# An S4D convolution beside a gated GLU: another way to the modes' exponential and angle, and skip weights first in their PSUM bank

## The chip, the cores and the metric

The kernel runs on one core of a Trainium2 chip. A core has five engines that run their own instruction queues side by side: TensorE (PE, with its weight loads PEld), VectorE (DVE), ScalarE (ACT), GpSimd (POOL) and SyncE (SP, which here only issues DMAs). Each queue is worked through in the order in which it was written. The metric is the device time of one execution in microseconds (us).

## The reference

The input x (2048 tokens, 448 channels) is normalised over its channels, and three terms are added: x itself, a state space convolution (branch A) and a gated linear unit (branch B).

```python
dt = jnp.exp(log_dt)
A = -jnp.exp(log_A_real) + 1j * A_imag
C = (C_real + 1j * C_imag) * dt[:, None]
P = jnp.exp((A * dt[:, None])[:, :, None] * pos[None, None, :])
K = 2.0 * jnp.einsum("dn,dnl->dl", C, P).real        # 448 x 2048, from 256 modes each
y = irfft(rfft(u_t, 2 * L) * rfft(K, 2 * L))[..., :L]
...
A_out = y + u * D_skip
h = sigmoid(xn @ w_gate) * (xn @ w_up)               # 1792 wide
return x + A_out + h @ w_down
```

For branch A each channel has 256 modes. Every mode has a magnitude that falls with the position, by exp(log_A_real) and dt, and a phase that grows with it. The complex weight C gives each mode a starting magnitude and a starting angle.

## The kernel before

Two streams of work are written as Python generators, `conv()` for branch A and `glu()` for branch B, and the main loop takes from whichever is further behind its share. A planner then fixes one order of instructions for every engine before the run, with a model of the times of its own. What is marked `hp` goes before other work as soon as the planner takes it for ready; `tc.issue_after` puts an instruction behind another one on its engine. On the chip each engine follows that order and waits where an input is late.

Branch B takes 14 columns of 128 of the hidden layer, in groups, and two halves of the tokens. `gate` does 22 matmuls for one column and 512 tokens into two PSUM tiles `gu` (L705). ACT makes `th` by Tanh from the first (L713), DVE makes `hf` from `th` and the second (L716), ACT rounds it to `hh` (L721), DVE takes the rest `hl` (L723). At the end of a group the matmuls `po` (L818) multiply with the down weights, and DVE adds the result to `acc` (L823). `po` and `gu` share four PSUM buffers (`tag="gu", bufs=4`). New weights come into `wraw` by DMA, ACT rounds them to `wh` (L755), DVE takes the rest `wl` (L759).

Branch A has three stages. `prep` works on the modes, in two halves of 224 channels (112 partitions, 512 modes on each), step by step in turn with the other half. In `exp` it computes the exponential of log_A_real and log_dt: the argument is clamped (L305), split into a whole power of two `ki` (L307) and a rest `fr` (L311 and L312), the rest goes through a Taylor polynomial of degree seven (L314 and six times L316), and the power is put into the exponent bits (L317, L318). ACT then makes Tanh and Exp of the results. For the angle of C, with a3 and b3 the absolute values of its parts, it divides the smaller by the larger (reciprocal on DVE in pieces of 128 columns, L322), takes Arctan on ACT after a table load (L375), and mends the octant and the signs (L385 to L391). Sine and cosine come from ACT (L386, L387). The phases go out to `ph_d`, in parts that matmuls can take without loss.

`kgen` then makes the kernel K in 56 chunks of 8 channels. For each chunk PE spreads the phases (`tr`, L538), ACT takes sines (`S`, L544 to L547), POOL makes powers of the magnitudes (`me`, `mf`, L516), DVE multiplies to `Et` and `Ft` (L598 to L600), and 64 small matmuls add up the modes into the PSUM bank `ko` (L612), four chunks to a bank. At the end of the fourth chunk one more matmul adds the skip weights `dm` to column 0 of each block (L622, in two passes), and ACT copies the bank to `ks` (L625). There is one `ko` bank, so the next group's first matmul into it waits for that copy. `spectra` multiplies the spectra and turns them back into the output.

Matmuls into PSUM add to what is there unless `start` is set, in which case they begin anew.

Of the kernel before, what the change touches and what calls it, by code (L numbers as in the profile page):

```python
# [21 lines left out]
N = 256  # L22
# [2 lines left out]
NB = 64  # L25
NK1 = 33
TWO_PI = 2.0 * math.pi
MAGIC = 1.5 * 2.0**23
NFT = F // 128
WK = 5.5  # L30
# [8 lines left out]
CP = D // 4  # L39
# [91 lines left out]
def s4d_glu_kernel(ctx, tc, io):  # L131
    nc = tc.nc
    hp = tc.high_priority
    v = nc.vector
# [16 lines left out]
    const = ctx.enter_context(tc.tile_pool(name="const", bufs=1, side="left"))  # L151
    ident = const.tile([128, 128], F32, name="ident")
    wx = const.tile([128, 64], F32, name="wx")
    wk = const.tile([128, 2, 128], F32, name="wk")[:, :, :64]
    hpi = const.tile([128, 1], F32, name="hpi")
    nc.gpsimd.memset(hpi, math.pi / 2)
    one = const.tile([128, 1], F32, name="one")
# [5 lines left out]
    dm = const.tile([128, D // 32, 8], F32, name="dm")  # L163
# [3 lines left out]
    junk = const.tile([128, 1], F32, name="junk")  # L167


    lim = const.tile([128, 2, 3], F32, name="lim")  # L170
    nc.gpsimd.memset(lim, -1.0)

# [127 lines left out]
                nc.scalar.dma_start(x1_d[:, r : r + 9 : 8], x1s_[p][64 * i : 64 * i + 64])  # L300
        yield 2 * WX

    def exp(ex, ki, fr, pl):

        v.tensor_scalar(ex, ex, lim[:CP, 0, 1:2], lim[:CP, 0, 2:3], ALU.min, ALU.max)  # L305
        yield
        nc.scalar.activation(ki, ex, AF.Identity, scale=1.0 / math.log(2.0))  # L307
        yield
        ln2h = 0.693359375
        ln2l = math.log(2.0) - ln2h  # L310
        v.scalar_tensor_tensor(fr, ki, -ln2h, ex, ALU.mult, ALU.add)  # L311
        v.scalar_tensor_tensor(fr, ki, -ln2l, fr, ALU.mult, ALU.add)  # L312
        cs = [1.0 / math.factorial(i) for i in range(8)]
        nc.scalar.activation(pl, fr, AF.Identity, scale=cs[7])  # L314
        for i in range(6, 0, -1):
            v.scalar_tensor_tensor(pl, pl, cs[i], fr, ALU.add, ALU.mult)  # L316
        v.tensor_scalar(ki, ki, 127.0, 8388608.0, ALU.add, ALU.mult)  # L317
        v.scalar_tensor_tensor(ex, pl, 1.0, ki.bitcast(F32), ALU.add, ALU.mult)  # L318

    def pieces(t):  # L320
        for i in range(0, 2 * N, 128):
            v.reciprocal(t[:, i : i + 128], t[:, i : i + 128])  # L322


    SF = [CP, 2 * N]
    three = lambda t: t[:, : 2 * N].rearrange("p (t n) -> p t n", t=2)
# [14 lines left out]
    def prep(pool, h, srcs):  # L341

        cr, ci, aim, ex = srcs
        new = lambda n, sh=SF, dt=F32: pool.tile(sh, dt, name=n, bufs=2)
        a3, b3, m3, w3, s3 = (new(n) for n in ("a3", "b3", "m3", "w3", "s3"))
# [6 lines left out]
        yield from exp(ex, ki, fr, pl)  # L352
        for i, c in enumerate((0.5, -1.0, 1.0 / TWO_PI, 2.0)):
            nc.scalar.activation(hdt[:, i], ex[:, 2 * N :], AF.Identity, scale=c)
        fr, pl, ki = fr[:, : 2 * N], pl[:, : 2 * N], ki[:, : 2 * N]
# [8 lines left out]
        nc.scalar.activation(pl, fr, AF.Identity, bias=one[:CP])  # L364
        exps[:] = [nc.scalar.activation(rc, rc, AF.Identity, bias=one[:CP])]
        yield
        v.scalar_tensor_tensor(m3, a3, 1e-37, b3, ALU.max, ALU.max)
        pieces(m3)
        v.tensor_tensor(w3, a3, b3, ALU.min)
        v.tensor_tensor(w3, w3, m3, ALU.mult)  # L370
        v.tensor_tensor(s3, a3, b3, ALU.subtract)
        nc.scalar.activation(s3, s3, AF.Sign)
        nc.scalar.activation(cr, cr, AF.Sign)
        with tc.issue_after(exps[0].ins):
            nc.scalar.activation(w3, w3, AF.Arctan)  # L375
        if h == 1:
# [5 lines left out]
        v.scalar_tensor_tensor(pl, fr, -1.0, rc, ALU.mult, ALU.mult)  # L382
        yield
        turn(pl, W1s[0], h)
        v.scalar_tensor_tensor(w3, w3, -math.pi / 4, s3, ALU.add, ALU.mult)  # L385
        nc.scalar.activation(m3, w3, AF.Sin, bias=qpi[:CP])  # L386
        nc.scalar.activation(s3, w3, AF.Sin, scale=-1.0, bias=qpi[:CP])  # L387
        v.scalar_tensor_tensor(w3, w3, -math.pi / 4, cr, ALU.add, ALU.mult)
        nc.scalar.activation(w3, w3, AF.Identity, bias=hpi[:CP])
        v.tensor_scalar(ci, ci, 0.0, -2.0 / TWO_PI, ALU.is_lt, ALU.mult)  # L390
        v.scalar_tensor_tensor(w3, ci, 1.0 / TWO_PI, w3, ALU.add, ALU.mult)  # L391
        yield

        scaled(fr, aim, 2)
# [62 lines left out]
    def kgen(pk):  # L457
# [124 lines left out]
        for g in range(NCK // NCH):  # L582
            for c in range(NCH):
                cn = g * NCH + c
                S = nxt
                me, mf = (m[:, 2 * DC * (c % 2) : 2 * DC * (c % 2) + 2 * DC] for m in mags)
                if c == 4 and NCH * (g + 1) < NCK:
                    with tc.issue_after(fts[0].ins):
                        powers(pms, g + 1, sins[0])
                if cn + 1 < NCK:  # L590
                    nxt = ahead(cn + 1)
                    if c % 2 == 1:
                        squares(coming[0])
# [6 lines left out]
                fts[:] = [v.tensor_tensor(Ft, two(mf), S[:, 3:5], ALU.mult)]  # L600
                if cn + 2 < NCK and c % 2 == 0:
                    coming = magnitudes(cn // 2 + 1)
                if c % 2 == 1:
                    mags = coming
                if cn % 4 == 0:
                    ko = psc[-1].tile([128, 8, 64], F32, name="ko", bufs=1)
                for q in range(2):
                    sl = 2 * (cn % 4) + q
                    for k in range(4):
                        h, cc = k // 2, k % 2  # L610
                        for j in range(4):
                            mm = nc.tensor.matmul(  # L612
                                ko[32 * j : 32 * j + 32, sl],
                                Ft[:, cc, DC * h + 4 * q + j],
                                Et[:, cc, DC * h + 4 * q + j],
                                start=(k == 0),
                                stop=(k == 3),
                                skip_group_check=True,
                            )
                if cn % 4 == 3:  # L620
                    ks = tl["ks"]
                    nc.tensor.matmul(  # L622
                        ko[:, :, 0], ident, dm[:, cn // 4], start=False, stop=True, skip_group_check=True
                    )
                    nc.scalar.copy(ks, ko)  # L625
# [392 lines left out]
    def conv():  # L1018
        with tc.tile_pool(name="psk", bufs=1, space=PSUM) as ps_, tc.tile_pool(
# [9 lines left out]
            with tc.tile_pool(name="pst", bufs=1, side="right", reuse_waits="tile") as pst:  # L1029
# [37 lines left out]
                skip = io["A_D_skip"].rearrange("(g s j) -> j g s", j=4, s=8)  # L1067
                for j in range(4):
                    nc.gpsimd.dma_start(dm[32 * j : 32 * j + 1], skip[j : j + 1])
                preps = [prep(pst, h, srcs[h]) for h in range(2)]  # L1070

                with tc.issue_after(xls[0].ins):
# [10 lines left out]
                n = 0  # L1083
# [71 lines left out]
```

## Time and profile before

| | |
|---|---|
| median of 3 runs | 723.75 us (722.47 to 728.36) |
| the profiled execution | 724.73 us, of which the span from first to last instruction is 722.9 us |
| mean granted clock of PE | 0.98 |
| HBM traffic | 72.13 MB read, 43.84 MB written |

In the profile a line such as L716 is a line of the kernel's text. In the view of waits a row gives who waited for whom, then the sum in us, the number of waits and the longest one. In the view of stretches a row gives the stretch, its length, the busy time and count of PE, PEld, DVE, ACT and POOL in that order, then PE's granted clock, the share of the DMA engines and the GB/s. In the timeline a row gives start, duration, engine, line, operation, output<-inputs and shapes, and in brackets how long the engine had been idle before and what ended that. In a row of grouped instructions the numbers after the bar are the busy time in us, the mean duration of one in ns, and the idle time before them. The 40 slices of the page, each of 18.1 us, show how the engines are loaded over time:

```profile
PE   3898999999999898999999999998999999999995
DVE  6899887689889899688488988978956555575543
ACT  3655966488688768795686786787642322313320
```

The modes' preparation lies in slices 2 to 6, `kgen` in slices 7 to 30, `spectra` after that.

### The profile page before, as it was taken

The page shows a single profiled execution, that of the slowest core. Times are in us where ns is not written, and L with a number is a line of the kernel's source. Part 1 is how long each engine was busy: PE and PEld are TensorE (multiplying, and loading weights), DVE is VectorE, ACT ScalarE, POOL GpSimd, SP SyncE. Part 2 cuts the span into 40 slices and gives each one's busy share as a digit, 9 for nine tenths or more (in the row PEclk, how much of TensorE's full clock was granted, in tenths as well). Part 3 has the DMA queues.
Part 4 walks back from the last instruction along what each step waited for, and adds up shares of the span by engine and source line. Part 5 has one row for each costly group of instructions (what it writes and reads, how often), then busy time and mean ns, then how long its engine had stood idle before and what let it go on. Part 6 is the DMA issues. An engine that isn't in the chain of part 4 may idle for free.

```text
span 722.9 us, 19254 instructions
## 1 busy us (share of the span) xinstructions
PE 676.9 (94%) x7780; PEld 532.5 (74%) x7780; DVE 553.6 (77%) x760; ACT 428.6 (59%) x678; POOL 361.9 (50%) x423
## 2 busy tenths in 40 slices
PE   3898999999999898999999999998999999999995
PEld 2676887778877785666778877877877777776784
DVE  6899887689889899688488988978956555575543
ACT  3655966488688768795686786787642322313320
POOL 2101177656997966775365697586944002441001
PEclk9998999999999999899999999999999999999998
DMA  9948164464254444556942332332269999999845
GB/s 215 240 123 228 39 201 159 149 198 139 63 167 136 136 114 135 151 162 185 261 133 83 106 111 75 96 114 84 61 183 270 267 255 241 252 258 216 200 121 161
DMA packets 102985, 117.25 MB, mean 162 GB/s; under 512 B 13232, under 2 KB 90864, under 8 KB 102896
## 3 DMA queue, kind: packets, MB, share of 16 engines
q1 hardware_dynamic: 78736, 91.87, 46.0%
q10 hardware_dynamic: 21584, 18.24, 9.5%
q0 software_dynamic: 2576, 5.90, 3.0%
q8 instruction: 62, 1.02, 0.6%
q14 instruction: 27, 0.22, 0.1%
HBM read 72.13 MB, written 43.84 MB: 160 GB/s over the span
## 4 chain that ended last, share of the span: by engine, by line
PE 63%; DVE 11%; ACT 9%; DMA 6%; issue 4%; SPq 2%; POOL 2%; ACTq 1%; POOLq 0%; DVEq 0%
PE gu L705 27%; PE po L818 14%; PE sp L900 7%; PE ko L612 5%; PE pv L927 4%; PE tr L538 3%; DVE Ft L600 2%; DVE Et L599 2%; DVE Et L598 2%; ACT S L547 1%; ACT S L545 1%; ACT S L544 1%; SPq L640 1%; DVE pm L452 1%; DMA ph<-ph_d 1%
## 5 line engine op out<-in xcount | busy, mean ns | idle before, releaser
L516 POOL TENSOR_TENSOR me<-me,pm 128x32 f32<-128x32 f32 (+1 forms) x168 | 138.2, 823 | 104.4 <-DVE Et L599 87.9
L516 POOL TENSOR_TENSOR mf<-mf,pm 128x64 f32<-128x64 f32 (+1 forms) x112 | 121.1, 1081 | 4.7
L705 PE MATMUL gu<-xh,wh 128*128 128x512 f32 x336 | 100.8, 407 | 0.9 <-ACT xh L221 0.7
L705 PE MATMUL gu<-xh,wl 128*128 128x512 f32 x336 | 97.3, 397 | 0.0
L705 PE MATMUL gu<-xl,wh 128*128 128x512 f32 x336 | 97.3, 396 | 0.0
L598 DVE TENSOR_TENSOR Et<-me,S 128x1024 f32<-128x1024 f32 x56 | 82.8, 1479 | 11.9 <-ACT S L547 11.8
L818 PE MATMUL po<-dh,hh 128*128 128x448 f32 x224 | 85.5, 382 | 4.3 <-DVE hf L716 2.9
L599 DVE TENSOR_TENSOR Et<-me,S 128x1024 f32<-128x1024 f32 x56 | 78.1, 1394 | 13.3 <-ACT me L529 6.3
L818 PE MATMUL po<-dl,hh 128*128 128x448 f32 x224 | 83.5, 373 | 0.0
L600 DVE TENSOR_TENSOR Ft<-mf,S 128x1024 f32<-128x1024 f32 x56 | 78.7, 1405 | 5.6 <-ACT S L547 2.7
L544 ACT ACTIVATE S<-tr 128x1024 f32<-128x1024 f32 x56 | 57.8, 1032 | 41.9 <-PE tr L538 41.2
L818 PE MATMUL po<-dh,hl 128*128 128x448 f32 x224 | 82.5, 371 | 0.1
L705 PEld LDWEIGHTS gu<-xh,wh 128*128 128x128 f32 x336 | 61.8, 191 | 21.9 <-issue 4.4
L612 PEld LDWEIGHTS ko<-Et,Ft 128*32 128x32 f32 x3584 | 53.8, 110 | 32.4 <-DVE Ft L600 13.7
L612 PE MATMUL ko<-Et,Ft 128*32 128x64 f32 x3584 | 64.6, 221 | 11.9 <-DVE Ft L600 11.4
L705 PEld LDWEIGHTS gu<-xh,wl 128*128 128x128 f32 x336 | 64.3, 192 | 14.9 <-DVE hf L716 0.7
L705 PEld LDWEIGHTS gu<-xl,wh 128*128 128x128 f32 x336 | 64.3, 192 | 13.8
L721 ACT CAST hh<-hf 128x512 fp32r<-128x512 f32 x56 | 35.0, 625 | 65.9 <-DVE hf L716 60.1
L716 DVE SCALAR_TENSOR_TENSOR hf<-th,gu 128x512 f32<-128x512 f32 x56 | 38.2, 682 | 36.9 <-PE gu L705 31.7
L547 ACT ACTIVATE S<-S,hpi 128x1024 f32<-128x1024 f32 x56 | 65.6, 1171 | 1.3 <-issue 1.3
L823 DVE SCALAR_TENSOR_TENSOR acc<-po,acc 128x448 f32<-128x448 f32 x80 | 48.0, 616 | 23.5 <-PE po L818 23.5
L723 DVE TENSOR_TENSOR hl<-hf,hh 128x512 fp32r<-128x512 f32 x56 | 47.7, 851 | 18.2 <-ACT hh L721 18.2
(209 smaller groups left out, 1281.4 us busy)
## 6 DMA issues: line engine op xcount, KB each, us to landing
sk_d<-sk ACTq DMA_DIRECT2D x14, 512.0 KB
sx<-x_d SPq DMA_DIRECT2D x32, 224.0 KB
skl<-sk_d SPq DMA_DIRECT2D x16, 448.0 KB
vp<-v_d SPq DMA_DIRECT2D x16, 448.0 KB
v_d<-vt SPq DMA_DIRECT2D x62, 112.0 KB
ph<-ph_d SPq DMA_DIRECT2D x224, 24.0 KB
wt_d<-wh SPq DMA_DIRECT2D x9, 512.0 KB
wt_d<-wl SPq DMA_DIRECT2D x9, 512.0 KB
```

The lines of the kernel that those rows point to most:

```text
L516: ins = nc.gpsimd.tensor_tensor(m[:, :, w + a : 2 * w : n], m[:, :, a:w:n], par(base + i).unsqueeze(2).to_broadcast([128, 4 * DC, w // n]) ...
L544: nc.scalar.activation(rows(cs), pv, AF.Abs)
L547: sins[:] = [nc.scalar.activation(cs, cs, AF.Sin, scale=-TWO_PI, bias=hpi)]
L598: v.tensor_tensor(Et[:, :, :, 32:64], two(me[:, :, 32:64]), S[:, 1::-1], ALU.mult)
L599: v.tensor_tensor(Et[:, :, :, 0:32], two(me[:, :, 0:32]), S[:, 1:3, :, ::-1], ALU.mult)
L600: fts[:] = [v.tensor_tensor(Ft, two(mf), S[:, 3:5], ALU.mult)]
L612: mm = nc.tensor.matmul(ko[32 * j : 32 * j + 32, sl], Ft[:, cc, DC * h + 4 * q + j], Et[:, cc, DC * h + 4 * q + j], start=(k == 0), stop=( ...
L705: glu_mm[:] = [nc.tensor.matmul(ps, a_, b_, start=(n == 0), stop=(n == len(mm) - 1))]
L723: v.tensor_tensor(hl, hf, hh, ALU.subtract)
L818: glu_mm[:] = [nc.tensor.matmul(po, a_[:, bs], w_, start=(n == 0), stop=(n == 3 * fc - 1))]
L823: v.scalar_tensor_tensor(acc[:, b], po, 0.5, acc[:, b], ALU.mult, ALU.add)
L900: mm = nc.tensor.matmul(to, tb[:kk, t, 64 * c : 64 * c + 64], rhs, start=True, stop=True, skip_group_check=True,)
```

## The change

It has three parts. In `exp` the polynomial becomes a product of two quadratics: one as a completed square of `fr` on ACT plus a constant, the other likewise with its own scale, and the factor `(fr + EXP_R) * fr` on DVE. The exponent bits are made by one ACT operation. `sq` uses the buffer of `m3`.

```diff
-        cs = [1.0 / math.factorial(i) for i in range(8)]
-        nc.scalar.activation(pl, fr, AF.Identity, scale=cs[7])
-        for i in range(6, 0, -1):
-            v.scalar_tensor_tensor(pl, pl, cs[i], fr, ALU.add, ALU.mult)
-        v.tensor_scalar(ki, ki, 127.0, 8388608.0, ALU.add, ALU.mult)
+        nc.scalar.activation(ki, ki, AF.Identity, scale=8388608.0, bias=bz[:CP, 3:4])
+        nc.scalar.activation(pl, fr, AF.Square, bias=bz[:CP, 0:1])
+        nc.scalar.activation(sq, fr, AF.Square, scale=EXP_S, bias=bz[:CP, 1:2])
+        nc.scalar.activation(sq, sq, AF.Identity, bias=bz[:CP, 2:3])
+        v.scalar_tensor_tensor(ex, fr, EXP_R, fr, ALU.add, ALU.mult)
+        v.scalar_tensor_tensor(pl, pl, EXP_K, sq, ALU.add, ALU.mult)
+        v.tensor_tensor(pl, pl, ex, ALU.mult)
         v.scalar_tensor_tensor(ex, pl, 1.0, ki.bitcast(F32), ALU.add, ALU.mult)
-
-    def pieces(t):
-        for i in range(0, 2 * N, 128):
-            v.reciprocal(t[:, i : i + 128], t[:, i : i + 128])
```

In `prep` the angle comes from (a3 - b3) / (a3 + b3), whose Arctan lies between -pi/4 and pi/4 and needs no mending of the octant. The division is a first guess of 1 / (a3 + b3) from the integer view of the number, on ACT, and refining steps on DVE and ACT.

```diff
-        v.scalar_tensor_tensor(m3, a3, 1e-37, b3, ALU.max, ALU.max)
-        pieces(m3)
-        v.tensor_tensor(w3, a3, b3, ALU.min)
-        v.tensor_tensor(w3, w3, m3, ALU.mult)
+        v.scalar_tensor_tensor(m3, a3, 1e-37, b3, ALU.max, ALU.add)
+        nc.scalar.activation(w3.bitcast(I32), m3.bitcast(I32), AF.Identity, scale=-1.0, bias=bz[:CP, 4:5])
         v.tensor_tensor(s3, a3, b3, ALU.subtract)
-        nc.scalar.activation(s3, s3, AF.Sign)
+        v.tensor_tensor(m3, m3, w3, ALU.mult)
+        v.scalar_tensor_tensor(w3, m3, -2.0, w3, ALU.add, ALU.mult)
+        nc.scalar.activation(m3, m3, AF.Square, scale=-1.0, bias=one[:CP])
+        nc.scalar.activation(m3, m3, AF.Square, bias=bz[:CP, 5:6])
+        v.scalar_tensor_tensor(w3, m3, 0.75, w3, ALU.add, ALU.mult)
+        v.tensor_tensor(w3, w3, s3, ALU.mult)
         nc.scalar.activation(cr, cr, AF.Sign)
+        nc.scalar.activation(cr, cr, AF.Identity, scale=1.0 / TWO_PI)
+        nc.scalar.activation(ci, ci, AF.Sign, bias=bz[:CP, 6:7])
...
-        v.scalar_tensor_tensor(w3, w3, -math.pi / 4, s3, ALU.add, ALU.mult)
         nc.scalar.activation(m3, w3, AF.Sin, bias=qpi[:CP])
         nc.scalar.activation(s3, w3, AF.Sin, scale=-1.0, bias=qpi[:CP])
         v.scalar_tensor_tensor(w3, w3, -math.pi / 4, cr, ALU.add, ALU.mult)
-        nc.scalar.activation(w3, w3, AF.Identity, bias=hpi[:CP])
-        v.tensor_scalar(ci, ci, 0.0, -2.0 / TWO_PI, ALU.is_lt, ALU.mult)
-        v.scalar_tensor_tensor(w3, ci, 1.0 / TWO_PI, w3, ALU.add, ALU.mult)
+        v.scalar_tensor_tensor(w3, w3, 0.25, ci, ALU.add, ALU.mult)
```

The constants for the biases lie in a new tile `bz` of seven columns, each set by one memset on POOL just before `prep` begins. In `kgen` the matmul of the skip weights is the first into its bank and has `start`; the 64 small ones of each chunk then only add.

```diff
                 if cn % 4 == 0:
                     ko = psc[-1].tile([128, 8, 64], F32, name="ko", bufs=1)
+                    nc.tensor.matmul(
+                        ko[:, :, 0], ident, dm[:, cn // 4], start=True, stop=False, skip_group_check=True
+                    )
...
-                                start=(k == 0),
+                                start=False,
...
                 if cn % 4 == 3:
                     ks = tl["ks"]
-                    nc.tensor.matmul(
-                        ko[:, :, 0], ident, dm[:, cn // 4], start=False, stop=True, skip_group_check=True
-                    )
                     nc.scalar.copy(ks, ko)
```

More of the change, by code (lines that the diff above doesn't have):

```diff
@@ L27 @@
 TWO_PI = 2.0 * math.pi
+EXP_A, EXP_B, EXP_C = -0.8713653843588568, 0.07851670935535562, 0.011531916857233048
+EXP_K, EXP_S, EXP_R = 15.06237810040421, 0.03720672317048426, 3.5715240100230314
 MAGIC = 1.5 * 2.0**23
@@ L167, in s4d_glu_kernel @@
     junk = const.tile([128, 1], F32, name="junk")
+    bz = const.tile([128, 7], F32, name="bz")
     lim = const.tile([128, 2, 3], F32, name="lim")
@@ L301, in x_spec, with exp @@
         yield 2 * WX
-    def exp(ex, ki, fr, pl):
+    def exp(ex, ki, fr, pl, sq):
         v.tensor_scalar(ex, ex, lim[:CP, 0, 1:2], lim[:CP, 0, 2:3], ALU.min, ALU.max)
@@ L344, in prep @@
         new = lambda n, sh=SF, dt=F32: pool.tile(sh, dt, name=n, bufs=2)
-        a3, b3, m3, w3, s3 = (new(n) for n in ("a3", "b3", "m3", "w3", "s3"))
+        a3, b3, w3, s3 = (new(n) for n in ("a3", "b3", "w3", "s3"))
+        sq = new("m3", [CP, 2 * N + 2])
+        m3 = sq[:, : 2 * N]
         ki, fr, pl = new("ki", [CP, 2 * N + 2], I32), new("fr", [CP, 2 * N + 2]), new("pl", [CP, 2 * N + 2])
@@ L351, in prep @@
         nc.scalar.activation(b3, ci, AF.Abs, scale=lim[:CP, 1, 0:1])
-        yield from exp(ex, ki, fr, pl)
+        yield from exp(ex, ki, fr, pl, sq)
         for i, c in enumerate((0.5, -1.0, 1.0 / TWO_PI, 2.0)):
@@ L1069, in conv @@
                     nc.gpsimd.dma_start(dm[32 * j : 32 * j + 1], skip[j : j + 1])
+                for i, c in enumerate((EXP_A, EXP_B, EXP_C, 127.0 * 8388608.0, float(0x7EF30000), 0.5, 1e-37)):
+                    nc.gpsimd.memset(bz[:, i : i + 1], c)
                 preps = [prep(pst, h, srcs[h]) for h in range(2)]
```

## The prediction

> **What bounds the kernel now.** I read the page's busy table first, then the waits of TensorE (PE), then the stretches, and last the instructions around the longest wait that this change can reach. "Within 1%" is used below for 716.5 to 731.0 us, that is 723.75 +- 7.24, about what a measurement of this kernel can tell from no change.
>
> ```profile
> PE 676.9 (94%) x7780; PEld 532.5 (74%) x7780; DVE 553.6 (77%) x760; ACT 428.6 (59%) x678; POOL 361.9 (50%) x423
> ```
>
> PE is busy for 676.9 of 722.9 us, and the change leaves its matmuls in number and shape as they are. So the time can fall only where PE stands still (46.0 us) or runs at a low clock. Freeing VectorE (DVE) is worth nothing in itself; it is worth what it takes out of PE's waits. Here are those waits, first of the stretch 0 to 130 us, then of 130 to 540 us:
>
> ```profile
> PE tr L212 <- DVE xn L270: 12.1, 1, 12.1
> PE po L818 <- DVE hf L716: 2.9, 1, 2.9
> PE gu L705 <- DVE xr L225: 2.7, 1, 2.7
> PE po L818 <- ACT hh L721: 1.4, 1, 1.4
> ...
> ```
> ```profile
> PE ko L612 <- DVE Ft L600: 11.4, 10, 2.3
> ...
> ```
>
> The 12.1 us are the start, before the change's first instruction. The modes' preparation (prep, and exp inside it) runs from about 24 to 104 us. The stretches there:
>
> ```profile
> 30.00:40.00 10.00, 7.29 (x25) 5.50 (x25) 9.94 (x19) 3.85 (x8) 1.14 (x1) 0.83 0.68 160
> 40.00:50.00 10.00, 10.00 (x68) 6.66 (x67) 10.00 (x27) 6.02 (x10) 0.00 (x0) 1.00 0.48 138
> 50.00:60.00 10.00, 10.00 (x69) 6.77 (x67) 10.00 (x17) 5.15 (x9) 2.08 (x1) 1.00 0.77 212
> 60.00:70.00 10.00, 7.09 (x26) 6.08 (x22) 9.57 (x18) 4.84 (x12) 0.20 (x1) 0.66 0.74 208
> 70.00:80.00 10.00, 10.00 (x53) 9.14 (x51) 7.88 (x18) 9.95 (x22) 0.00 (x0) 1.00 0.39 98
> ```
>
> DVE (third busy number) has no room from 30 to 70 us, ScalarE (ACT, fourth) has 20.1 us of room there (40 less 3.85, 6.02, 5.15 and 4.84) and none from 70 to 80. From 40 to 60 PE runs without a gap; in 60:70 it loses 2.9 us of busy time and its granted clock is 0.66. That one hole, seen on DVE and on PE:
>
> ```profile
> 53.13 1.76 DVE L322 RECIPROCAL m<-m 112x128 f32<-112x128 f32 x2
> 54.80 0.63 DVE L723 TENSOR_TENSOR hl<-hf,hh 128x512 fp32r<-128x512 f32 x1
> 55.35 4.19 DVE L322 RECIPROCAL m<-m 112x128 f32<-112x128 f32 x5
> 59.45 1.17 DVE L759 TENSOR_TENSOR wl<-wraw,wh 128x1024 fp32r<-128x1024 f32 x1
> 60.53 0.94 DVE L322 RECIPROCAL m<-m 112x128 f32<-112x128 f32 x1
> 61.39 1.23 DVE L316 SCALAR_TENSOR_TENSOR pl<-pl,fr 112x514 f32<-112x514 f32 x2
> ...
> 62.61 0.68 DVE L716 SCALAR_TENSOR_TENSOR hf<-th,gu 128x512 f32<-128x512 f32 x1
> ```
> ```profile
> 53.58 0.84 PE L705 MATMUL gu<-xl,wh 128*128 128x512 f32 x3
> ...
> 59.96 0.47 PE L818 MATMUL po<-dh,hl 128*128 128x448 f32 x1
> 63.35 0.74 PE L818 MATMUL po<-dh,hh 128*128 128x448 f32 x1 [2.91 <-DVE hf L716]
> 63.88 0.57 PE L818 MATMUL po<-dl,hh 128*128 128x448 f32 x1
> ...
> 69.11 0.38 PE L818 MATMUL po<-dh,hl 128*128 128x448 f32 x1
> 69.32 0.36 PE L818 MATMUL po<-dh,hh 128*128 128x448 f32 x1
> ```
>
> The gate's matmuls that feed hf end at 54.42 (53.58 + 0.84), and hf runs at 62.61: for 8.2 us it stands in DVE's queue behind six reciprocals, wl, hl and two steps of the exponential's polynomial, with not one idle moment of DVE between. po shares its four PSUM buffers with gu, and hf is what empties gu, so PE stops at 60.44 and goes on at 63.35. Then it pays again: 15 matmuls start between 63.35 and 69.11, 0.384 us apart, where one at full rate takes 0.21 (69.11 to 69.32).
>
> **The change, part by part.** The costs are distances between starts on a full engine, since instructions overlap at their ends.
>
> ```profile
> 40.53 0.42 DVE L317 TENSOR_SCALAR ki<-ki 112x514 int32<-112x514 int32 x1
> 40.87 0.68 DVE L316 SCALAR_TENSOR_TENSOR pl<-pl,fr 112x514 f32<-112x514 f32 x1
> 41.47 0.57 DVE L249 BATCH_NORM_AGGREGATE mv<-st 128x2 f32<-128x6 f32 x7
> ```
> ```profile
> 32.73 0.68 DVE L312 SCALAR_TENSOR_TENSOR fr<-ki,fr 112x514 f32<-112x514 int32 x1
> ```
> ```profile
> 68.61 0.30 ACT L354 ACTIVATE hdt<-ex 112x2 f32<-112x2 f32 x2
> ...
> 71.88 0.71 ACT L364 ACTIVATE pl<-fr,one 112x512 f32<-112x512 f32 x1
> 72.49 0.71 ACT L365 ACTIVATE ki<-ki,one 112x512 f32<-112x512 f32 x1
> ...
> 76.06 1.28 ACT L375 ACT_TABLE_LOAD   x1
> ```
> ```profile
> L156 POOL MEMSET hpi<- 128x1 f32 x1 | 0.1, 98 | 0.3 <-POOLq L1141 0.3
> ```
>
> A full DVE operation of this size costs 0.60 us (40.87 to 41.47), a tensor_scalar 0.34 (40.53 to 40.87). The eight reciprocals cost 1.67 + 4.10 + 0.86 = 6.63 us by their starts above. An ACT operation with a bias from a tile costs 0.61 (71.88 to 72.49); I take the few without one at the same price.
>
> The exponential, for each of the two halves: DVE loses six L316 and one L317 and gains three full operations: -6 x 0.60 - 0.34 + 3 x 0.60 = -2.14. The angle: it loses four reciprocals (3.31), the minimum (0.60), L385 (0.60) and L390 (0.34), and gains three full operations (1.80): -3.05. The two halves together: -10.4 us of DVE, 6.6 of it by the reciprocals. ACT, each half: the exponential gains four and loses one, the angle gains five (the Identity on the integer view, two Squares, the scaling of cr, the Sign of ci) and loses two. Net six, for two halves 12 x 0.61 = 7.3 us more. They need fr, which is ready at 33.41 (32.73 + 0.68), and m3; both lie in the stretch in which ACT has 20.1 us free, so I cost them at nothing. If that cover were gone they would cost up to 7.3 us on the ACT chain that begins with L354 at 68.61, behind which PE had no wait over 1.4 us. Whether Square needs another table load is not in the trace for that stage; Abs, Sign and Identity ran there without one. The bounds are 0 and two swaps, there and back, of 1.3 us each for each half (the load at 76.06 took 1.28), 5.1 us that the same room would hide; I take 0. The seven memsets on POOL (0.1 us each by the memsets of one column in that stage) come before ACT's first new operation and ahead of nothing that PE waits for: 0 to 0.7, taken as 0.
>
> "ScalarE: Activation LUTs" of the Trainium skill (section Rules for kernel authors) says to use VectorE, not ScalarE, for adds and multiplies, being up to about three times faster per element in bf16. In fp32 here the trace has 0.60 against 0.61 us, so by this trace the move itself costs nothing; if ACT's share were three times DVE's, an estimate from that page, the 12 operations would be 21.6 us and would just not fit into ACT's room.
>
> What this does to the hole: without the 6.63 us of reciprocals alone hf starts at 55.98, 4.5 us before PE comes to its po at 60.44. Even if half of the reciprocals' time were taken by other operations moved in front of hf, it would be in time. So the 2.91 us of waiting go, and with them the slow matmuls: 15 x (0.384 - 0.21) = 2.61. **Sum: 5.5 us.** What is late next? The wl of the following weights moves up with the same queue, and PE was busy for all of 70 to 80, so that work simply runs 5.5 us earlier. The second half of prep starts up to 10.4 us earlier, being behind the exponential on DVE.
>
> On the clock, "TensorE: Matmul & The Clock Gate" (Part 1: The HAM clock gate) of the Trainium skill says that about 3.4 us of idleness brings the half rate and about 3.4 us of work ends it. The trace differs: half rate came after 2.91 us, and lasted 5.8. By that page alone the hole would cost 2.9 us, and the kernel would come out at 720.8.
>
> The skip weights: the two passes of their matmul move from the end of each group of four chunks to its front, with start taken from the first ko matmul and given to them. PE's work is the same. They now wait for the bank, that is for the copy ks of the group before, and everything behind them on PE waits too. First and last of the thirteen such handovers, PE above and ACT below:
>
> ```profile
> 163.48 0.39 PE L622 MATMUL ko<-dm,ident 128*128 128x8 f32 x2
> ...
> 169.97 0.71 PE L612 MATMUL ko<-Et,Ft 128*32 128x64 f32 x36
> ```
> ```profile
> 165.20 0.58 ACT L625 COPY ks<-ko 128x512 f32<-128x512 f32 x1
> ```
> ```profile
> 511.14 0.39 PE L622 MATMUL ko<-dm,ident 128*128 128x8 f32 x2
> ...
> 516.89 0.52 PE L612 MATMUL ko<-Et,Ft 128*32 128x64 f32 x21
> ```
> ```profile
> 511.56 0.59 ACT L625 COPY ks<-ko 128x512 f32<-128x512 f32 x1 [2.38 <-PE ko L622]
> ```
>
> The copy ended at 165.78 and 512.15, and the next ko, which needs the same bank, came 4.2 and 4.7 us later. Placed anywhere in those 4 us the new matmul waits for nothing. Placed at once behind the old group it would stand 1.91 and 0.62 us. On the other side, ks is freed of 0.3 us of matmul ahead of it, which nothing on PE waits for. I take 0; the bounds are +16.4 us (13 x 1.27, the mean of the two) and nothing below zero.
>
> **How it stands to the median.** The profiled execution took 724.73 us, 1.8 more than its span and 0.98 more than the median 723.75. 724.73 - 5.5 = 719.2 there; for the median 718.2.
>
> **The rivals.** (1) The hole stays. The order on DVE is fixed by the planner before the run. If it fills the freed time with other preparation in front of hf, hf is as late as now, and the time is 723 to 724. For it: hf at 62.61 was behind four kinds of work, not the reciprocals alone. Against: DVE's supply ahead of the ACT chain is finite and falls by 10.4 us. Chance 0.20. (2) It clears more. If the modes' chunks, which start after prep, gain the 4.9 us by which prep moves ahead more than PE, the 1.4 us behind hh and about half of the 11.4 us of waiting for Ft go as well: 718.2 - 7.1 = 711.1. Against: DVE's load per chunk is unchanged, so a lead may be used up within a few chunks. Chance 0.20. (3) The slower side: the skip matmul is placed right behind the old group and PE stands for the copy: 718.2 + 16.4 = 734.6. It decides from 5.5 / 13 = 0.42 us for each handover on. For it: ACT came to the first copy 1.33 us after the matmul's end. Against: the 4.2 and 4.7 us of room. Chance 0.14, of which 0.12 over 731.0. (4) Only the wait goes and the low clock stays, from other thin work such as the small L281 matmuls before it: 720.8; chance 0.05, inside the forecast's range.
>
> **How the numbers follow.** The forecast has 0.46 with (4) in it, its own range 714 to 722, because a new order moves the ten waits for Ft too, the longest of which is 2.3 us. A third of it, 0.15, lies under 716.5; with rival 2 that makes 0.35 for faster. Slower: 0.12. Within 1%: 0.53. The range is 710 to 727: it takes in the forecast, rival 1, most of rival 2, and a few short waits of rival 3, and leaves out about 0.18.
>
> **What would show it.** Right: no RECIPROCAL on DVE; hf of the fifth gate within 2 us of its last gu matmul; no gap on PE near 60 and granted clock 1.00 in 60:70; the Arctan load about 8 to 10 us earlier than 76.06; no second table load before it; ACT still not the releaser of any PE wait before 110. Wrong: a PE wait released by hf or th between 50 and 80; waits at the skip matmul's line released by ks; waits for Ft adding up to more than 17 us, which would eat the gain.

## The result, and the profile after

The changed kernel takes 734.24 us (median of 4 runs, 727.5 to 737.85) against 723.11 us for the kernel before beside it: ratio 1.0117, interval 1.0072 to 1.0162. In a second comparison, with twelve runs, it took 732.56 against 726.29: 1.0080 (1.0053 to 1.0107). It is slower by about 6 to 9 us, where 5.5 us of gain were forecast. A ratio here is an estimate over the runs of both kernels with a 95% interval; it is not the quotient of the two medians, which is 1.0154 in the first comparison. Runs more than 1.5% above the fastest of their kernel count as slow and are left out of the ratios, which concerns one of twelve runs with the skip weights alone (736.09 us) and two of twelve with the sines behind Silu (737.19 and 740.44), whose ratio of 1.0028 would be about 1.005 with them.

The profiled execution took 737.85 us, 736.1 of them span, and was the longest of the four. Some 5 of the 13.2 us by which its span is longer than the one before arise at 640 to 660 us, where PE was busy for 17.12 of 20 us at a granted clock of 0.86 (19.02 at 1.00 in the kernel before); that is an estimate, 1.9 us of busy time and 0.14 of 20 us of clock. The same kernel profiled again took 732.74 us and was busy there for 19.96 us at 1.00, so this part belongs to the one execution. Its busy times, and its waits of TensorE (PE) from 0 to 130 us and from 130 to 540:

```profile
PE 683.5 (93%) x7780; PEld 535.9 (73%) x7780; DVE 547.2 (74%) x744; ACT 438.2 (60%) x691; POOL 359.1 (49%) x430
```
```profile
PE tr L215 <- DVE xn L273: 12.7, 1, 12.7
PE ko L442 <- ACT x1ab L299: 5.7, 1, 5.7
PE gu L709 <- DVE xr L228: 2.8, 1, 2.8
PE gu L709 <- ACT xh L224: 1.4, 2, 1.3
...
```
```profile
PE ko L619 <- DVE Ft L604: 9.2, 9, 2.9
...
```

The instructions moved as counted: 16 fewer on VectorE (760 to 744), 13 more on ScalarE (678 to 691: the twelve of the sum, and one table load). The wait behind hf is gone. In its stead stands a longer one, 5.7 us, for ScalarE's copy out of the PSUM banks of the first stage. The stretches (PE is the first busy number, ACT the fourth):

```profile
50.00:60.00 10.00, 9.35 (x47) 5.89 (x45) 8.82 (x19) 10.00 (x24) 0.00 (x0) 1.00 0.43 133
60.00:70.00 10.00, 10.00 (x52) 7.63 (x49) 8.80 (x13) 10.00 (x20) 1.35 (x2) 0.83 0.67 200
70.00:80.00 10.00, 6.14 (x29) 4.92 (x28) 6.93 (x12) 9.91 (x14) 0.00 (x0) 1.00 0.77 209
80.00:90.00 10.00, 8.15 (x30) 7.11 (x31) 9.68 (x14) 6.10 (x14) 4.12 (x3) 0.66 0.63 164
```

The two engines have changed places. VectorE has room from 50 to 80 us; ScalarE, which was half idle from 50 to 70, now has none up to 80. PE is full in 60:70, as forecast, loses 3.9 us in 70:80, and runs 80:90 at a granted clock of 0.66. The hole begins some 16 us later (76.20 against 60.44) and is almost twice as long, and the same low clock comes behind it. ScalarE around that place, and what PE stands for:

```profile
49.13 0.49 ACT L356 ACTIVATE hdt<-ex 112x2 f32<-112x2 f32 x4 [1.97 <-DVE z L262]
...
70.69 1.28 ACT L382 ACT_TABLE_LOAD   x1
...
74.18 1.28 ACT L392 ACT_TABLE_LOAD   x1
75.47 0.72 ACT L392 ACTIVATE m<-w,qpi 112x512 f32<-112x512 f32 x1
76.11 0.70 ACT L393 ACTIVATE s<-w,qpi 112x512 f32<-112x512 f32 x1
...
77.75 0.89 ACT L297 COPY x1ab<-tr 128x896 f32<-128x896 f32 x1
78.66 1.28 ACT L384 ACT_TABLE_LOAD   x1
...
81.70 0.53 ACT L299 COPY x1ab<-kp 128x448 f32<-128x448 f32 x1
```
```profile
68.64 0.54 PE L284 MATMUL kp<-xn,wx 32*64 32x448 f32 x2
...
75.83 0.36 PE L822 MATMUL po<-dh,hl 128*128 128x448 f32 x1
81.85 0.63 PE L442 MATMUL ko<-ident,pl 112*128 112x112 f32 x2 [5.65 <-ACT x1ab L299]
```

The first stage's last matmuls end at 69.18, and the last of their three copies runs at 81.70. ScalarE is not idle in between: it works through the modes' chain, which the order on the engine puts first: Arctan, the sines of the first half, and three table loads where the kernel before had two. The chain itself (hdt, Tanh) begins at 49.13. In the kernel before it began at 68.61, behind the last of those copies.

The gate whose hf made the hole at 60 us, in four rows: its th in the kernel before, then in the changed kernel its last matmuls, its th and its hf:

```profile
53.24 0.59 ACT L713 ACTIVATE th<-gu 128x512 f32<-128x512 f32 x1
```
```profile
54.85 0.84 PE L709 MATMUL gu<-xl,wh 128*128 128x512 f32 x3
```
```profile
59.89 0.59 ACT L717 ACTIVATE th<-gu 128x512 f32<-128x512 f32 x1
```
```profile
60.63 0.68 DVE L720 SCALAR_TENSOR_TENSOR hf<-th,gu 128x512 f32<-128x512 f32 x1
```

The skip matmul waits for nothing. Its line in the view by tile:

```profile
L611 PE MATMUL ko<-dm,ident x28: 170/214/256, 128.2 to 522.2; 128*128 128x8 f32 x28
...
its engine sat idle before it (us, times) until:
who waited for it (us, times):
```

Both lists are empty.

### The profile page after: what moved, and what is told of

Read it like the earlier page. It is cut to its first block, busy times and chain, and to the rows that moved or that the text cites. A ratio compares the mean times of both kernels' runs of the same rounds, so it can differ in the third digit from the quotient of the medians.

```text
span 736.1 us, 19249 instructions
## 1 busy us (share of the span) xinstructions
PE 683.5 (93%) x7780; PEld 535.9 (73%) x7780; DVE 547.2 (74%) x744; ACT 438.2 (60%) x691; POOL 359.1 (49%) x430
## 4 chain that ended last, share of the span: by engine, by line
PE 40%; DVE 9%; ACT 2%; issue 2%; POOL 2%; DMA 0%; ACTq 0%; POOLq 0%; DVEq 0%
PE gu L709 17%; PE sp L904 7%; PE po L822 6%; PE pv L931 4%; PE ko L619 3%; DVE Et L602 2%; DVE Et L603 2%; DVE Ft L604 2%; PE tr L542 1%; POOL me L520 1%; DVE pm L456 1%; DVE acc L827 1%; PE pv L966 1%; PE kp L566 1%; ACT S L551 1%
## 5 line engine op out<-in xcount | busy, mean ns | idle before, releaser
L603 DVE TENSOR_TENSOR Et<-me,S 128x1024 f32<-128x1024 f32 x56 | 80.2, 1432 | 17.9 <-ACT me L533 11.7
L602 DVE TENSOR_TENSOR Et<-me,S 128x1024 f32<-128x1024 f32 x56 | 84.1, 1503 | 7.8 <-ACT S L551 7.6
L619 PEld LDWEIGHTS ko<-Et,Ft 128*32 128x32 f32 x3584 | 55.9, 112 | 31.3 <-DVE Ft L604 13.5
L619 PE MATMUL ko<-Et,Ft 128*32 128x64 f32 x3584 | 67.2, 225 | 11.2 <-DVE Ft L604 9.2
L717 ACT ACTIVATE th<-gu 128x512 f32<-128x512 f32 x56 | 33.7, 602 | 57.6 <-PE gu L709 56.9
```

What stands on the lines that cost most here:

```text
L619: mm = nc.tensor.matmul(ko[32 * j : 32 * j + 32, sl], Ft[:, cc, DC * h + 4 * q + j], Et[:, cc, DC * h + 4 * q + j], start=False, stop=(k = ...
```

## The experiments

All ratios are to the kernel before, run beside each on the same chip, with 95% intervals. The expectations speak of three theories. Theory 1: ScalarE's preparation chain comes some 19 us earlier, runs into the first stage's copies, and PE waits for a PSUM bank. Theory 2: the skip matmul costs the time. Theory 3: nothing costs anything by itself, only the later order was reshuffled. Later on, Theory C is Theory 1's collision, and Theory L the third table load.

**One part alone.** The skip weights first, on the kernel before:

```diff
 ko = psc[-1].tile([128, 8, 64], F32, name="ko", bufs=1)
+nc.tensor.matmul(
+    ko[:, :, 0], ident, dm[:, cn // 4], start=True, stop=False, skip_group_check=True
+)
...
-    start=(k == 0),
+    start=False,
...
-nc.tensor.matmul(
-    ko[:, :, 0], ident, dm[:, cn // 4], start=False, stop=True, skip_group_check=True
-)
```

> The kernel before with the skip weights first in their bank as the only edit. Theory 1 (ScalarE's preparation chain starts some 19 us earlier, runs into the copies of the convolution's first stage, and TensorE waits for a PSUM bank at the first transposes of prep): nothing of that is in this kernel, so 719 to 727 us, the wait of 2.9 us near 60 us still there, none at the skip matmul. Theory 2 (the skip matmul in front costs the time): 730 us or more, with waits at the skip matmul or at ko.

Measured: 1.0027 (1.0001 to 1.0052), with the wait of 2.9 us behind hf as before. The new exponential alone, with the old angle and the skip weights last:

> The kernel before with the new exponential only (old angle with its reciprocals, skip weights last). VectorE loses 4.3 us and ScalarE gains 3.7. Theory 1: ScalarE's chain (the first Tanh of prep, at 69.4 us before and 49.5 us in the changed kernel) starts at 60 to 66 us, the wait at the transposes stays under 2 us, time 720 to 727. Theory 3 (only the new order of the later stages costs the time, whatever is edited): 728 or more with no large wait before 130 us.

Measured: 1.0019 (0.9992 to 1.0047). The first row of ScalarE's chain in it:

```profile
48.21 0.58 ACT L361 ACTIVATE hdt<-ex 112x2 f32<-112x2 f32 x5 [1.41 <-DVE ex L323]
```

The chain begins as early as in the changed kernel, and not at 60 to 66 us, although all eight reciprocals are still there. Yet no single wait of PE from 50 to 130 us reaches 1.7 us: an early chain alone does not stop PE. The new angle alone:

> The kernel before with the new angle only (Taylor polynomial kept, skip weights last). VectorE loses 6.1 us. Theory 1: the first Tanh of prep at 58 to 64 us, that is half way, a wait at the transposes of 0 to 4 us, time 720 to 732. Theory 3: 728 or more with no large wait before 130 us.

Measured: 1.0136 (1.0095 to 1.0178), a median of 734.06 us and so above the range expected, and the changed kernel with the skip weights last again:

> The changed kernel with the skip weights put back to the end of their bank. Theory 1: as slow as the changed kernel, 730 to 738 us, with a TensorE wait of 4 to 6 us at the first transposes of prep near 76 us. Theory 2: back to 718 to 725 us.

Measured: 1.0079 (1.0051 to 1.0107), the same as with them first (1.0080). So the skip weights are not the cause, and the angle is the costly part. This run also speaks against Theory 3: in its trace PE's order from 140 us on is that of the kernel before (some 120 of the 7780 matmuls stand elsewhere, all of them earlier), and the loss is there all the same. In the angle alone PE's waits from 50 us on are of another kind than in the whole change:

```profile
PE po L820 <- DVE acc L825: 4.0, 2, 2.4
PE po L820 <- ACT hh L723: 1.9, 1, 1.9
...
```

**What makes the stop of 5.7 us.** The sines held behind Silu, so that Silu's set is fetched before them and two loads are enough:

```diff
-nc.scalar.activation(junk[:CP], w3[:, 0:1], AF.Silu)
+silu[:] = [nc.scalar.activation(junk[:CP], w3[:, 0:1], AF.Silu)]
...
+with tc.issue_after(silu[0].ins):
     nc.scalar.activation(m3, w3, AF.Sin, bias=qpi[:CP])
     nc.scalar.activation(s3, w3, AF.Sin, scale=-1.0, bias=qpi[:CP])
```

> The changed kernel with the sines of both halves put behind the Silu on ScalarE, so that one table load serves both (in the changed kernel the first half's sines came ahead of it and a third load of 1.28 us was made). Theory 1 (ScalarE is full from 50 to 83 us and the bank of the first transposes is copied out late): the wait at the transposes shrinks from 5.65 us by 1.3 to about 4.4, time 729 to 735. Theory 3 (only the later order matters): no relation.

Measured: 1.0028 (0.9999 to 1.0058). Two loads are left, and the stop is shorter by 1.4 us:

```profile
PE ko L443 <- ACT x1ab L299: 4.3, 1, 4.3
...
```

The first stage one step earlier, so that its copies stand ahead of the chain:

```diff
-if n in (2, 3):
-    if n == 2:
+if n in (1, 2):
+    if n == 1:
...
-yield from x_spec([xns[n - 2][:, b + i] for i in range(2)], 4 * (n - 2) + b)
+yield from x_spec([xns[n - 1][:, b + i] for i in range(2)], 4 * (n - 1) + b)
```

> The changed kernel with the first stage of the convolution (its matmuls and the copies out of PSUM) written one step of prep earlier, ahead of prep's chain on ScalarE. Theory 1: the copies no longer stand among the chain, the wait of 5.65 us at the first transposes goes, and with it the low clock behind it: 8 us less than the changed kernel, 720 to 727. If the time stays at 730 or more with that wait gone, the later stages hold the loss (theory 3).

Measured: 1.0046 (1.0017 to 1.0075), some 2.5 us less than the changed kernel where 8 were expected. The stop at the transposes (ko L442) is gone, and one of 2.7 us stands at the first stage itself:

```profile
PE tr L284 <- ACT x1ab L297: 2.7, 1, 2.7
...
```

Three of ScalarE's operations of each half on VectorE:

```diff
-nc.scalar.activation(ki, ki, AF.Identity, scale=8388608.0, bias=bz[:CP, 3:4])
+v.tensor_scalar(ki, ki, 127.0, 8388608.0, ALU.add, ALU.mult)
-nc.scalar.activation(sq, sq, AF.Identity, bias=bz[:CP, 2:3])
+v.tensor_scalar(sq, sq, EXP_C, None, ALU.add)
-nc.scalar.activation(cr, cr, AF.Identity, scale=1.0 / TWO_PI)
+v.tensor_scalar(cr, cr, 1.0 / TWO_PI, None, ALU.mult)
```

> The changed kernel with three of ScalarE's new operations of each half (exponent bits, constant of the second square, scale of the sign) put on VectorE as tensor_scalar: 6 x 0.61 = 3.7 us less on ScalarE, 6 x 0.34 = 2.0 more on VectorE. Theory 1: the wait at the transposes falls to between 1 and 4 us, time 726 to 733. A rival (VectorE is still what holds the stage): no gain or a loss, 733 or more.

Measured: 1.0075 (1.0045 to 1.0105): next to nothing, although the stop shrank as expected, to two of 1.8 and 1.9 us. A shorter stop need not make a shorter kernel. All three together, and then also the skip weights last:

> The changed kernel with all three edits (Silu ahead of the sines, first stage one step earlier, three operations of each half on VectorE). Theory 1: no wait of TensorE over 1 us between 40 and 110 us, time 716 to 725, at or under the kernel before. Theory 3: 728 or more in spite of it.

> The kernel with the three reliefs (sines behind Silu, three ScalarE operations of each half on VectorE, first stage one step early), and in addition the skip weights last in their bank again. If the skip matmul's new place has a small price of its own (1.0027 when it was done alone), the ratio to the kernel before comes to 0.996 to 0.999; if that 0.0027 was only the order of other work being reshuffled, it stays at 0.999 to 1.003 like the kernel without this edit (1.0000).

Measured: 1.0000 (0.9972 to 1.0029) and 1.0018 (0.9991 to 1.0045). The loss is given back, no gain shows, and 0.0027 for the skip weights does not show again. In the first of the two PE stands elsewhere: 3.7 us for VectorE's acc up to 71 us, where no wait over 1 us was expected, and 2.1 us for the phases' DMA up to 119 us.

**Is there a gain without ScalarE's part?** The kernel before with its reciprocals left out, then the kernel before with twelve idle Squares on ScalarE and VectorE's work untouched, and beside them the changed kernel once more:

```diff
-pieces(m3)
```
```diff
 yield from exp(ex, ki, fr, pl)
+for _ in range(3):
+    nc.scalar.activation(dmy, fr[:, : 2 * N], AF.Square)
...
+for _ in range(3):
+    nc.scalar.activation(dmy, m3, AF.Square)
 pieces(m3)
```

> The kernel before with its eight DVE reciprocals left out and nothing put in their place (the angle is then computed from wrong numbers; all other work is there): VectorE is 6.6 us shorter ahead of hf and ScalarE gets no operation more. If the forecast's own step holds (the hole at 60 us and the low clock behind it are owed to the reciprocals, and only ScalarE's added work takes the gain back), the hole of 2.9 us at 60 is gone, nothing takes its place before 110 us, and the ratio is 0.992 to 0.996. If the earlier preparation is the cause by itself (what is freed comes earlier and collides with the first stage, whoever does it), TensorE stops elsewhere between 60 and 90 us for 2 us or more and the ratio is 0.998 to 1.006.

> The kernel before with twelve ScalarE operations more (six of each half, 112x512 Squares into a tile that nobody reads, three behind fr and three behind m3); VectorE's work and all results are as before. If ScalarE's added load costs the time by itself, TensorE waits for ScalarE's copies (a wait on ACT x1ab, xh or hh of 2 us or more before 90 us) and the ratio is 1.004 to 1.010. If the load alone fits into the 20 us that ScalarE has free, and it takes the earlier preparation to make it collide, no such wait of 2 us shows and the ratio is 0.998 to 1.002.

> The changed kernel as it is, beside the others on one chip: 1.007 to 1.016 by the first comparison. The three table loads and the stop at 76 to 82 us of 5 us or more show again if they come from the order of the instructions and not from one disturbed execution.

Measured: without reciprocals 1.0008 (0.9987 to 1.0028); with idle Squares 1.0026 (0.9999 to 1.0052); the changed kernel 1.0080, its stop 5.6 us again. The first lies in what was expected if the earlier preparation collides whoever does it. The second lies between its two expectations, and no wait for ScalarE's copies in it reaches 2 us (the longest is 1.6). The first is the most telling run of the study. PE, VectorE and ScalarE of the kernel without reciprocals at the old hole:

```profile
56.12 0.84 PE L704 MATMUL gu<-xl,wh 128*128 128x512 f32 x3
...
57.90 0.98 PE L281 MATMUL tr<-xn,wx 32*64 32x448 f32 x8
61.03 0.84 PE L281 MATMUL ko<-xn,wx 32*64 32x448 f32 x2 [2.14 <-ACT x1c L296]
```
```profile
58.73 0.67 DVE L715 SCALAR_TENSOR_TENSOR hf<-th,gu 128x512 f32<-128x512 f32 x1
```
```profile
59.44 0.62 ACT L720 CAST hh<-hf 128x512 fp32r<-128x512 f32 x1 [4.18 <-DVE hf L715]
...
59.96 0.59 ACT L712 ACTIVATE th<-gu 128x512 f32<-128x512 f32 x1
60.45 0.52 ACT L296 COPY x1c<-ko 128x448 f32<-128x448 f32 x1
```
```profile
60.00:70.00 10.00, 8.97 (x31) 6.64 (x32) 6.37 (x17) 8.63 (x25) 0.20 (x1) 0.66 0.75 217
```

hf no longer holds po up. But ScalarE stands idle for 4.18 us for hf, in the order of its queue, and the copy of the first stage's bank is two places behind. So PE stops for 2.1 us instead of 2.9, two microseconds earlier than before, and the granted clock of 60:70 is 0.66 as before. hf itself came 5.4 us after its gate's last matmuls (53.30 to 58.73) against 8.2 before, 2.8 us sooner and not 6.63. And PE waits 2.6 us for the phases at the modes' first chunk, which the kernel before begins at 115.74 without waiting:

```profile
111.57 0.71 PE L537 MATMUL tr<-sel,ph 128*128 128x512 f32 x2 [2.63 <-DMA ph<-ph_d]
```

PE's waits from 50 to 130 us add up to 4.7 us, against 4.5 in the kernel before.

**Chain or load?** So far the kernels at 1.0046 and above had three table loads, the others two; in most of those with a loss the copies were late as well. Four runs to part the two: a third load alone in the kernel before (first diff); the angle alone with the sines behind Silu, as above; and the changed kernel with its chain held behind the first stage's copies (second diff), with three loads and with two:

```diff
+nc.scalar.activation(junk[:CP], w3[:, 0:1], AF.Sin)
 nc.scalar.activation(junk[:CP], w3[:, 0:1], AF.Silu)
```

```diff
+    cps[:] = [nc.scalar.copy(x1s_[1][:, j], kk[j][:, :D])]
...
+yield
+with tc.issue_after(cps[0].ins):
     for i, c in enumerate((0.5, -1.0, 1.0 / TWO_PI, 2.0)):
...
```

> The kernel before with one table load more: a Sin of a single column ahead of the Silu that fetches the last set, so that ScalarE loads Arctan's, Sin's and Silu's set (three) instead of two; all else is as before. In the ten variants so far and the changed kernel, the ones with three loads come to 1.0046 to 1.0136 and the ones with two to 1.0000 to 1.0028. If the third load by itself is the cause (Theory L), the ratio is 1.004 or more here too. If it only costs where first-stage copies stand behind it (Theory C, the collision), its 1.28 us falls in a place where no copy of the first stage waits any more, and the ratio is 0.998 to 1.003.

> The new angle alone (1.0136 when it ran with three table loads), with the sines held behind Silu so that two loads are left. Theory L: 1.000 to 1.005. Theory C: the last first-stage copies still stand in the middle of ScalarE's preparation chain, between 70 and 80 us, so 1.006 to 1.012 remains.

> The changed kernel, with the time-step scales, Tanh and Exp of both halves (and what follows from them) held back on ScalarE behind the copies of the first stage; three table loads stay. Theory C: TensorE's stop of 5.6 us at 75 to 82 us is gone, the low clock behind it too, and the ratio falls from 1.008 to 1.003 or less. Theory L: three loads, so 1.005 or more, whether the stop is there or not.

> Both: the chain held behind the first stage's copies, and two table loads. Theory C: the same as with the hold alone, within 0.002. Theory L: 0.003 or more below the hold alone. If the change's shorter VectorE work is worth anything once ScalarE is out of the way, this is below 0.998; if TensorE then stops at another place for what it saves (as the kernel without reciprocals did), it is 0.998 to 1.003.

Measured: 1.0029 (1.0002 to 1.0055), 1.0112 (1.0076 to 1.0148), 1.0206 (1.0162 to 1.0251) and 1.0188 (1.0143 to 1.0234). The first decides little: its profiled execution lost 4.4 us behind hf at 59 us, ahead of the three loads of this stage. The second is what Theory C expected. The third does take the stop away, yet loses more than the change itself. Its stretch 270:350, long after preparation, and that of the kernel before:

```profile
270.00:350.00 80.00, 72.13 (x856) 46.27 (x859) 55.62 (x65) 54.10 (x89) 48.66 (x58) 0.83 0.53 149
```
```profile
270.00:350.00 80.00, 75.97 (x980) 51.73 (x978) 65.48 (x81) 63.30 (x103) 50.82 (x63) 0.94 0.60 172
```

The extra `yield` counts as a step of the convolution side, and the order in which convolution and GLU are woven together is made from that count: PE's whole later order came out otherwise, with 3.8 us less of PE's busy time in that stretch and a clock of 0.83. So the same two again, with no step added:

```diff
-yield WP
+if n != 3:
+    yield WP
```

> The chain held back behind the first stage's copies as before, but with no step added to the conversion's count, so that TensorE's order after the first 17 hundredths of its instructions is that of the changed kernel but for a dozen places (in the run before, the added step put all the later work in another order, and the loss stood at 270 to 350 us). Three table loads stay. Theory C (collision): no stop of 5.6 us at 75 to 82 us, and 1.000 to 1.004. Theory L (third load): 1.005 or more. If the late chain itself costs something later, TensorE waits beyond 90 us for what the chain feeds (ph, W, GG or Ft) by 2 us or more than in the changed kernel.

> The same with two table loads. Theory C: within 0.002 of the run with three. Theory L: 0.003 or more below it. Below 0.998 would show the forecast's gain, with ScalarE out of the way; 0.998 to 1.004 shows that TensorE stops elsewhere for what is saved.

Measured: 1.0045 (1.0021 to 1.0070) with three loads, 1.0006 (0.9976 to 1.0036) with two. The first lies between the two theories' ranges; the difference, 0.0039, is what Theory L expected. PE's waits from 50 to 130 us, with two:

```profile
PE tr L284 <- ACT x1ab L297: 2.9, 1, 2.9
PE po L825 <- ACT hh L728: 2.1, 1, 2.1
```

The stop at 75 is gone in both, the loss with it in the second; and at 61 us stands a stop as long as that of the kernel before. What ScalarE does there (kernel with two loads):

```profile
59.58 1.34 ACT L376 ACTIVATE m<-m,one 112x512 f32<-112x512 f32 x2 [0.56 <-DVE hf L723]
60.82 1.32 ACT L377 ACTIVATE m<-m,bz 112x512 f32<-112x512 f32 x2
62.04 0.60 ACT L728 CAST hh<-hf 128x512 fp32r<-128x512 f32 x1
...
63.04 0.89 ACT L297 COPY x1ab<-tr 128x896 f32<-128x896 f32 x1
```

Four of the new Squares, 2.46 us, stand ahead of hh and of the copy that PE waits for. What was taken from VectorE's queue stands in ScalarE's, in front of the same consumer.

None of these kernels beats the kernel before: the best, 1.0000 and 1.0006, are equal to it.

## Why the prediction was wrong

- **VectorE's side was counted right.** Sixteen operations fewer, no reciprocal, no wait of PE behind hf at 60, PE full in 60:70. The clock there was not 1.00 but 0.83. What the count could not give was the order: with the reciprocals out and nothing added, hf began at 58.73, not at 55.98.
- **The step that failed first: "both lie in the stretch in which ACT has 20.1 us free, so I cost them at nothing".** Free time of an engine that works in order is not room: what counts is who stands behind the new operation. th of the fifth gate ran at 53.24 in the kernel before; in the changed kernel the gate's matmuls end at 55.69 and th runs at 59.89, behind the chain, so hf comes 4.9 us after the matmuls (60.63) and not within 2. As load alone the twelve operations cost little (1.0026, with 1.000 inside the interval, idle Squares in the same stretch); their places in the order cost more.
- **"The second half of prep starts up to 10.4 us earlier" was mis-sized, and read as harmless.** It started 19.5 us earlier (68.61 to 49.13). What did this is the shorter polynomial, which is now finished ahead of the angle's work on VectorE, where its last steps had stood behind the reciprocals: the new exponential alone, with all reciprocals, begins the chain at 48.21, the kernel without reciprocals only at 62.35. That alone does no harm (1.0019). With the new angle's operations in the same queue the chain ran into the first stage's copies instead of following them. Holding it back behind the copies takes the ratio from 1.0080 to 1.0045, 2.5 us, though the two intervals overlap.
- **The table loads were looked for at the wrong operation.** I weighed a swap for Square; there is none, nor a second load ahead of Arctan. The load for Arctan came 5.4 us earlier (70.69), not 8 to 10. But the sines of the first half now come ahead of Silu, and the order of first uses makes three loads of 1.28 us. Four pairs of kernels differ in this load and hardly else: changed kernel (1.0080 and 1.0028), angle alone (1.0136, 1.0112), the two holds (1.0206, 1.0188 and 1.0045, 1.0006). The mean difference is 0.0033, 2.4 us. The first and the last difference just reach their own uncertainty, the two others lie well within it, and in the first two pairs the runs lie in different comparisons. That all four have one sign, and that a third load alone cost 0.0029, makes the load's part likely and does not show it. PE's order in each pair is the same but for a few places. Load and collision together, the last kernel against the changed one, make 0.0074, 5.4 us: nearly all of the 0.0080. Here the intervals are well apart, so that the two together make the loss is shown, and only their shares are not.
- **"What is late next?" had the wrong answer.** I took PE to run on 5.5 us earlier, since it was busy for all of 70 to 80. Taking out the reciprocals and adding nothing gains nothing (1.0008), because hh and behind it the bank's copy stand in ScalarE's queue waiting for the same hf, and because PE then waits for the phases at the modes' first chunk. The hole was owed to the whole line from VectorE over ScalarE to the bank. Of the low clock behind it, 2.6 of the 5.5 us, half stayed in the changed kernel although the hole went: what rival 4 said, with a chance of 0.05.
- **The skip weights were judged right.** No wait in 28 passes; rival 3's mechanism did not happen, although its time, 734.6, is close to the one measured. That is chance. Alone they cost 1.0027, an interval that just misses 1; in the two pairs of kernels that differ in them alone (1.0080 and 1.0079, 1.0000 and 1.0018) nothing of it shows.
- **Ft waits** add up to 9.2 us, under the 17 that would have eaten a gain. "ACT still not the releaser of any PE wait before 110" is the sign that came out wrong, and it named the cause. (Word for word it was untrue of the kernel before too, where ScalarE's xh released a wait of 0.7 us at 29.72.)

Open: where in the run the third load's 2.4 us are lost when the collision is away. One execution of each of the two last kernels, 730.0 and 729.1 us of span, doesn't show it. Why the angle alone is slower than the whole change is seen only in its waits (VectorE's acc, with the old, long polynomial beside the new angle); no run took that apart. Nor does a run show which of the angle's operations on ScalarE it takes to make the early chain collide.

## What to carry to other kernels

When a stall is removed, follow the waiting engine's other inputs and name the next one in time, with the queue it stands in; if it comes after less than the expected gain, the gain ends there. Before moving work to an engine with idle time, list what is queued on it behind the new operations and who waits for that; and check in which order functions of different table sets will now be used first. In a kernel whose order is planned from counted steps, one step more can reorder everything after it, so compare an experiment's order with that of the kernel it came from before reading its time.

## What the runs showed of the hardware

PE's clock fell with hardly an idle hole. In the changed kernel PE at 54 to 62 us:

```profile
53.95 0.84 PE L709 MATMUL gu<-xh,wl 128*128 128x512 f32 x3
54.62 0.39 PE L709 MATMUL gu<-xr,wl 128*128 128x512 f32 x1
...
57.35 0.98 PE L284 MATMUL tr<-xn,wx 32*64 32x448 f32 x8 [0.52 <-ACT x1c L297]
58.38 0.97 PE L284 MATMUL ko<-xn,wx 32*64 32x448 f32 x4
59.42 0.97 PE L284 MATMUL kp<-xn,wx 32*64 32x448 f32 x4
60.32 1.19 PE L709 MATMUL gu<-xh,wl 128*128 128x512 f32 x2
61.31 0.63 PE L709 MATMUL gu<-xr,wl 128*128 128x512 f32 x1
```

PE stood idle for 0.52 us only, but for 3 us it ran the first stage's matmuls, which use a 32x64 part of its array, one bank after the other. The matmuls that follow are slow: 0.50 us each by their starts (60.32 to 61.31, two), where three of their kind took 0.22 each before (53.95 to 54.62). And 60:70 has a granted clock of 0.83: if the low rate is half, as these two spacings suggest, that is an estimate of 3.4 us at half rate in 10. That the thin use of the array is the cause is argued; no run varied it alone. "TensorE: Matmul & The Clock Gate" of the Trainium skill (Part 1: The HAM clock gate) names an idle window of about 3.4 us as the cause of half rate. The trace differs in that half rate came here after a stretch that was thinly used and hardly idle; it lasted 3.4 us, as long as that page's window.
